# One more pair of heads in cluster order, scatters dealt out by 20 to three steps, and block loads in a fused routing-attention and FFN kernel

## The chip, the cores and the metric

The kernel runs on one NeuronCore of a Trainium2 chip. The metric is device microseconds of one execution, lower is better. Five engines work side by side, each through its own instructions in order: TensorE (PE in the profile; PEld are its weight loads), VectorE (DVE), ScalarE (ACT), GpSimd (POOL) and SyncE (SP), which issues most DMAs.

## The reference

Attention of 4 batches, 8 heads, 768 tokens and head size 64, in which a query sees only keys of its own cluster, followed by a feed-forward network (FFN) with a leaky activation.

```python
q_assign = np.argmax(np.einsum('bhsd,hcd->bhsc', q_n, c_n), axis=-1)   # 16 clusters
k_assign = np.argmax(np.einsum('bhsd,hcd->bhsc', k_n, c_n), axis=-1)
mask = q_assign[:, :, :, None] == k_assign[:, :, None, :]
scores = np.where(mask, scale * np.matmul(q, k.transpose(0, 1, 3, 2)), -1000000000.0)
attn = np.exp(scores - np.max(scores, axis=-1, keepdims=True))
attn = attn / (np.sum(attn, axis=-1, keepdims=True) + 1e-09)
x = np.matmul(attn, v)            # then (B,H,S,D) -> (B*S, H*D) = 3072 x 512
h = x @ w_in                      # 512 x 2048
out = (np.maximum(h, 0.0) + alpha * np.minimum(h, 0.0)) @ w_out   # 2048 x 512
```

## The kernel before, in words

**Pairs and steps.** Two heads fill the 128 partitions; with 4 pairs to a batch there are 16 pairs, numbered 0 to 15. The list `steps` says in which order they are worked on. An ordinary pair is done in two halves of 384 queries (`half` 0 and 1), each in three steps of two key chunks. From step 24 (`TOGETHER`) on, three steps make a group: at its first step (s == 0) TensorE makes the scores of half of the chunks (`score`, L781), sums the denominators of the group before (`total`, L891), weighs the values of the group before (`weigh`, L936, or `weigh_near`, L969), and makes the rest of the scores. ScalarE takes the exponentials (L799, L802), VectorE masks them (`mask`, L822) and adds them up.

**Pairs in cluster order.** From pair `NO` = 10 on, tokens of a pair are sorted by cluster, so that a key chunk meets only a window of the queries: 224, 320 or 384 instead of 768. Such a pair has `half` None and takes one group of three steps in place of two groups. Sorting costs: features turned by VectorE (L565), similarities (`order_sims`, L573), argmax, a scan (L587), two small matmuls (`order_begins`, L599), ranks. Then tokens of q, k and v are loaded into one of two stages (`order_stage`, SP) and 24 indirect DMAs of POOL write them to a scratch in DRAM (`order_scatter`, L673). `order_load` reads them back in order. Afterwards the outcome goes back: transposes (`to_rows`, L999), 12 indirect DMAs (`put_back`, L1008), a load (`fetch_back`, L1020) and `turn_back` (L1027).

**The scatter queue.** The deque `sorting` holds stages and scatters. In every slot (one of 12 places in a group where pieces are put out) up to `room` scatters leave it: one, two in the first step, none where the group before is a pair in cluster order, since its put-backs are then on POOL. With each goes a `pace`: ScalarE copies one element (L649) and POOL copies that (L650), so POOL can't run ahead of ScalarE. The tokens have 8 buffers.

**FFN as filling.** A batch half of the FFN is a list of 28 pieces: 16 of `hidden` (L1063) and 12 of `final` (L1081), each 8 instructions here. They are dealt out evenly over a block of steps between two entries of `begun_at`: batch 1's second half over steps 48 to 59, batch 2's over 60 to 65 and 66 to 77. `kept` holds a few back over the block's end. The last batch's FFN follows after the last step, in a Strassen form (`last_pieces`, products L1241 and L1297, additions L1176, slopes L1181).

**Batch 0.** In the first 24 steps the two weight matrices come as 64-bit words through five raw tiles and are converted by VectorE, ScalarE and POOL (`convert`, L247 to L271). Pairs 0 to 3 are turned into features by TensorE (`prep_features`, L354, copied by ScalarE in L358); later pairs arrive in blocks of 32 features and VectorE turns these (`prep_blocks`, L364). Mask terms of batch 0 ride on the score matmul (L790).

**Order by hand.** `prep_at` and `load_at` say at which step and slot a preparation or load is put out, `ORDERS` at which step each pair's sorting begins, and `later(k, ...)` puts a piece k ticks (slots) on.

```python
    ORDERS = [26, 29, 35, 38, 41, 50]
            room = 0 if steps[u - SB][1] is None else 1 + (s == 0)
        return {NS: 12, begun_at[-2]: 8, begun_at[-3]: 2}.get(block_end(u), 0)
```

Of the kernel before, what the change touches and what calls it, by code (L numbers as in the profile page):

```python
# [19 lines left out]
P = 128  # L20
# [3 lines left out]
def kernel(  # L24
# [77 lines left out]


    pairs = [(b, hp) for b in range(B) for hp in range(NCH)]
    NO = WHOLE * NCH - 2
    NP = len(pairs)
    raw_qk, vts = {}, {}

    Q = 32

    def load(n):

        b, hp = pairs[n]
        for w, src in enumerate((q, k)):
            raw = inp.tile([P, 2, NJ, D], FP32, name="qk")
            if n < NCH:
                nc.sync.dma_start(
                    out=raw.rearrange("p h j d -> p h (j d)"),  # L120
                    in_=src[b, 2 * hp:2 * hp + 2].rearrange("h (p j) d -> p h (j d)",
                                                            j=NJ))
            for h in range(2):
                rows = src[b, 2 * hp + h]
                for x in range(D // Q if n >= NCH else 0):
                    r = h * D + x * Q
                    nc.sync.dma_start(
                        out=raw.rearrange("p h j d -> p (h j d)")[r:r + Q, :].rearrange(
                            "p (t i) -> p t i", i=Q),
                        in_=rows[:, x * Q:(x + 1) * Q].rearrange("(t p) i -> p t i", p=Q))  # L130
            raw_qk[n, w] = raw

    def load_v(n):
        b, hp = pairs[n]
# [189 lines left out]
    lowest = const.tile([P, B], FP32, name="lowest")  # L324
    highest = const.tile([P, B], FP32, name="highest")
    WORDS = [float((127 + e) * 2 ** 23) for e in (-50, 40)]
    kept_of = [0]

    def inverse(n, half):

        if pairs[n][0] > kept_of[0]:
            check_inverses()
        return inverses[:, (2 * n + half) % (2 * NCH), :]

    def check_inverses():
# [343 lines left out]
    def order_load(n):  # L679
        assert len(scattered[n]) == 2 * NX  # L680
        whole = scratch.pop(n)[0]
        found = sorts["order"].tile([P, 2, NJ, 1], I32, name="found")
        for h in range(2):
            r0 = 2 * h * S
            nc.sync.dma_start(out=found[:, h], in_=whole.bitcast(I32)[
# [40 lines left out]
    for b in range(B):  # L726
        whole = [n for n in range(b * NCH, (b + 1) * NCH) if n >= NO]
        rest = [n for n in range(b * NCH, (b + 1) * NCH) if n < NO]
        begun_at.append(len(steps))
        steps += [(n, None, s) for n in whole for s in range(SB)]  # L730
        for half in range(2) if rest else ():
            if half:
                begun_at.append(len(steps))
            steps += [(n, half, s) for n in rest for s in range(SB)]
            feeds[len(steps)] = b, half
    begun_at.append(len(steps))
    assert NJ == 6 and GROUP == 2

# [274 lines left out]
    def fetch_back(n, whole):  # L1013

        b, hp = pairs[n]
        raw = inp.tile([P, 2, NJ, D], FP32, name="qk").rearrange("p h j d -> p (h j d)")
        for h in range(2):
            for x in range(D // Q):
                r = h * D + x * Q
                nc.sync.dma_start(  # L1020
                    out=raw[r:r + Q, :].rearrange("p (t i) -> p t i", i=Q),
                    in_=whole[h * S:(h + 1) * S, x * Q:(x + 1) * Q].rearrange(
                        "(t p) i -> p t i", p=Q))

        def turn_back():
            for half in range(2):
                nc.vector.transpose(out=x_tile(b, half)[:, hp, :],  # L1027
                                    in_=raw[:, half * HS:(half + 1) * HS])
        later(4 if n == NP - 1 else 9, turn_back)

    def x_tile(b, half):
        if (b, half) not in xTs:
# [106 lines left out]
    def last_pieces():  # L1139
# [93 lines left out]
        def hidden(x):  # L1233
# [33 lines left out]

            def p3():
                plus(g_of(f1, 1), product("e", "S4", x_of(1, 1), False))
                slopes(f1)  # L1270

            def p7():
                plus(g_of(f2, 1), product("a", "S3", x_of(1, 0), False))
                late.append(p4)
                if x % 2 == 0 and x:
                    g_sums(x - 2)
# [86 lines left out]
    FREE = SLOTS * SB - 3  # L1363


    ORDERS = [26, 29, 35, 38, 41, 50]
    prep_at, load_at = {}, {}
    for (n, half), u in start_of.items():
        def at(step, slot, piece):
            prep_at.setdefault((step, slot), []).append(piece)  # L1370
        if half is None:
            t = ORDERS[n - NO]
            load_at.setdefault(t, []).append(lambda n=n: load(n))
            for i in range(2):
                at(t + 1, FIRST + i, lambda n=n, i=i: order_features(n, i))
            at(t + 2, 2, lambda n=n: order_sims(n))
            load_at.setdefault(u - (3 if n == NO + 1 else 4), []).append(
                lambda n=n: order_load(n))
            at(u - 4, 0, lambda n=n: prep_clusters(n))
            for i in range(2):  # L1380
# [2 lines left out]
            continue  # L1383
        if half == 0:
            if n < NCH:
                if n > 1:
                    load_at.setdefault(max(u - 7, 0), []).append(lambda n=n: load(n))
                if n > 0:
                    load_at.setdefault(max(u - 6, 0), []).append(lambda n=n: load_v(n))
            else:  # L1390
                load_at.setdefault(u - 9, []).append(lambda n=n: load(n))
                load_at.setdefault(u - 7, []).append(lambda n=n: load_v(n))
            if n < NCH:
                for g in range(len(groups)):
                    at(u - 4, FIRST + g, lambda n=n, g=g: prep_features(n, g))
            else:
                for w in range(2):
                    at(u - 7, FIRST + w, lambda n=n, w=w: prep_blocks(n, w))
            at(u - (3 if n < NCH else 5 if u - 6 < TOGETHER else 6), FIRST,
               lambda n=n: prep_sims(n))  # L1400
            if n >= NCH:
                at(u - 4, FIRST if u - 4 < TOGETHER else 0, lambda n=n: prep_clusters(n))
        if n < NCH:
# [19 lines left out]
    def feed_block(u):  # L1423
        if u == NS:
# [2 lines left out]
                ffn[i] = lambda piece=ffn[i], p=p: (piece(), w_in_sums(p))  # L1427
            ffn.extend(last_pieces())
            return
        ffn.extend(ffn_pieces(*feeds[u]))  # L1430

    def kept(u):


        return {NS: 12, begun_at[-2]: 8, begun_at[-3]: 2}.get(block_end(u), 0)

    def block_end(u):
        return min(x for x in begun_at if x > u)
# [59 lines left out]
    for u in range(TOGETHER, NS + 1):  # L1498
# [54 lines left out]
        for i in slots:  # L1553
# [4 lines left out]
            places = (block_end(u) - block_start(u)) // SB * FREE  # L1558
            pieces = len(ffn) - kept(u) + -whole * (places - 1 - at_slot) // places
            todo.popleft()()  # L1560
            room = 0 if steps[u - SB][1] is None else 1 + (s == 0)
            if room and sorting:
                pace()
            while sorting and room:
# [231 lines left out]
```

## Time and profile before

| What | Value |
|---|---|
| median of 3 runs | 943.94 us (943.76 to 946.52) |
| the profiled execution | 944.23 us, its span 942.5 us |
| PE, DVE, ACT, POOL busy | 924.1, 663.5, 265.9, 351.2 us |
| FFN matmuls L1063, L1081 | 257.7 us (768), 254.4 us (576) |
| score matmuls L781 into sps, values L936 into vps | 88.6 us (480), 87.4 us (480) |
| scatters L673, put-backs L1008 | 155.4 us (144), 74.9 us (72) |
| pace copies L649 on ACT, L650 on POOL | 27.2 us, 55.5 us (196 each) |

Busy time is the union of an engine's instructions; the mean of one can be longer than its share, since instructions overlap in the pipeline. A nc.tensor.matmul in fp32 appears as two instructions. A wait is told as "engine line <- engine line: us, times, longest". The groups of three steps can be found in the timeline by the bursts of L781: from step 24 on they start at 196.6, 223.3, 262.4, 288.1, 323.1, 351.0, 384.4, 412.9, 445.5 (step 48, pair 10), 470.1, 508.2, 531.9, 562.2, 605.6, 643.8 (step 66, pair 12), 671.0, 696.4 and 721.6 us.

### The profile page before, as it was taken

What the parts mean: (1) busy time and instruction counts of PE and PEld (TensorE: products, weight loads), DVE (VectorE), ACT (ScalarE), POOL (GpSimd) and SP (SyncE); (2) the same over time, 40 slices, a digit from 0 to 9 for tenths busy, and PEclk for the clock granted to TensorE, in tenths of its full rate; (3) what the DMA queues carried; (4) which work ended last, traced back from release to release, by engine and by line L of the source; (5) the groups of instructions that cost most, each with busy time, mean ns of one, the idle gap of its engine ahead of it and who ended that gap; (6) DMA issues with size and microseconds to landing.
All of it is one profiled execution on the core that took longest, in us unless ns stands there. A gap on an engine that the chain in (4) does not pass through costs nothing.

```text
span 942.5 us, 11891 instructions
## 1 busy us (share of the span) xinstructions
PE 924.1 (98%) x3995; PEld 496.5 (53%) x3995; DVE 663.5 (70%) x1247; ACT 265.9 (28%) x658; POOL 351.2 (37%) x529
## 2 busy tenths in 40 slices
PE   8999999999999999999999999999999999999997
PEld 5534444445455454454544545545455555556886
DVE  5797788799679589698995955456888535698100
ACT  5764444323123032331322322223133121221000
POOL 2333222200016576467534686364256670000000
PEclk9999999999999999999999999999999999999999
DMA  8333658039001645165920134333441112000000
GB/s 297 125 127 96 146 130 149 18 59 198 1 6 53 159 87 133 47 120 131 155 52 12 43 80 101 63 67 62 93 75 34 32 37 53 1 0 1 23 23 26
DMA packets 209668, 73.38 MB, mean 78 GB/s; under 512 B 194288, under 2 KB 198080, under 8 KB 209600
## 3 DMA queue, kind: packets, MB, share of 16 engines
q1 hardware_dynamic: 201840, 60.35, 29.2%
q0 software_dynamic: 6912, 11.81, 4.1%
q8 instruction: 33, 0.54, 0.2%
q10 hardware_dynamic: 848, 0.39, 0.2%
q14 instruction: 35, 0.29, 0.1%
HBM read 49.89 MB, written 22.28 MB: 77 GB/s over the span
## 4 chain that ended last, share of the span: by engine, by line
PE 87%; DVE 6%; SPq 2%; DMA 2%; issue 1%; POOL 1%; ACT 1%; ACTq 0%; DVEq 0%; POOLq 0%
PE fps L1081 26%; PE fps L1063 25%; PE vps L936 7%; PE sps L781 7%; PE sps L1297 4%; PE sps L1241 4%; PE fps L781 2%; PE vps L1297 2%; PE vps L1241 2%; PE fps L1297 1%; PE fps L1241 1%; PE sps L790 1%; PE vps L969 1%; PE mps L969 1%; PE mps L381 1%
## 5 line engine op out<-in xcount | busy, mean ns | idle before, releaser
L1063 PE MATMUL fps<-xT,w_in_sb 128*128 128x384 f32 x768 | 257.7, 490 | 0.0
L1081 PE MATMUL fps<-w_out_sb,gT 128*128 128x512 f32 x576 | 254.4, 595 | 1.1 <-DVE gT L1055 1.1
L1063 PEld LDWEIGHTS fps<-xT,w_in_sb 128*128 128x128 f32 x768 | 142.8, 190 | 102.6 <-issue 3.8
L1081 PEld LDWEIGHTS fps<-w_out_sb,gT 128*128 128x128 f32 x576 | 107.5, 190 | 133.4 <-issue 123.0
L673 POOL DMA_INDIRECT scratch<-stage,off x144 | 155.4, 1079 | 49.7 <-issue 25.1
L650 POOL COPY paced<-pace 1x1 f32<-1x1 f32 x196 | 55.5, 283 | 202.3 <-ACT pace L649 201.5
L1069 ACT COPY gT<-fps 128x384 f32<-128x384 f32 x96 | 46.0, 479 | 215.6 <-PE fps L1063 215.6
L1055 DVE SCALAR_TENSOR_TENSOR gT<-gT,alpha 128x384 f32<-128x384 f32 x96 | 61.3, 648 | 50.4 <-ACT gT L1069 50.3
L781 PE MATMUL sps<-qkT 64*128 64x384 f32 (+1 forms) x480 | 88.6, 487 | 0.0
L1008 POOL DMA_INDIRECT back<-rows,found x72 | 74.9, 1040 | 18.2 <-issue 16.1
L802 ACT ACTIVATE E<-sps 128x768 f32<-128x768 f32 (+1 forms) x78 | 57.9, 790 | 59.4 <-PE sps L790 38.8
L781 PEld LDWEIGHTS sps<-qkT 64*128 64x128 f32 x480 | 42.7, 186 | 40.5 <-issue 15.0
L822 DVE SCALAR_TENSOR_TENSOR more<-aq,key,more 128x384 f32<-128x384 bf16 (+2 forms) x120 | 63.0, 584 | 1.2 <-ACT more L799 1.1
L936 PE MATMUL vps<-E,vt 128*64 128x384 f32 x316 | 58.6, 495 | 1.4 <-DVE xT L1039 1.4
L904 DVE RECIPROCAL inverses<-mps 64x12 f32<-64x12 f32 (+1 forms) x44 | 10.9, 248 | 58.5 <-PE mps L891 58.1
L822 DVE SCALAR_TENSOR_TENSOR E<-aq,key,E 128x384 f32<-128x384 bf16 (+2 forms) x96 | 50.2, 577 | 1.9 <-ACT E L799 1.8
L271 POOL TENSOR_TENSOR w_in_sb<-w_in_sb,power 128x512 f32<-128x512 f32 x16 | 25.1, 1573 | 67.8 <-DVE w_in_sb L268 67.8
L832 DVE TENSOR_TENSOR acc<-acc,E 128x768 f32<-128x768 f32 x37 | 35.3, 953 | 14.7 <-ACT E L802 13.6
L271 POOL TENSOR_TENSOR w_out_sb<-w_out_sb,power 128x512 f32<-128x512 f32 x16 | 22.9, 1434 | 57.3 <-DVE w_out_sb L268 57.3
L802 ACT ACTIVATE more<-sps 128x768 f32<-128x768 f32 (+1 forms) x42 | 31.1, 775 | 33.1 <-PE sps L781 32.0
L1087 ACT COPY y<-fps 128x512 f32<-128x512 f32 x18 | 10.6, 586 | 99.1 <-PE fps L1081 99.1
L1089 DVE TENSOR_TENSOR y<-y,fps 128x512 f32<-128x512 f32 x24 | 16.4, 683 | 29.1 <-PE fps L1081 29.1
(283 smaller groups left out, 1167.2 us busy)
## 6 DMA issues: line engine op xcount, KB each, us to landing
raw<-in_moe_w_in_dram SPq DMA_DIRECT2D x16, 512.0 KB
raw<-in_moe_w_out_dram SPq DMA_DIRECT2D x16, 512.0 KB
out_dram<-y SPq DMA_DIRECT2D x21, 256.0 KB
qk<-in_q_dram SPq DMA_DIRECT2D x48, 96.0 KB
qk<-in_k_dram SPq DMA_DIRECT2D x48, 96.0 KB
qk<-scratch SPq DMA_DIRECT2D x48, 96.0 KB
w_in_kept<-w_in_sb SPq DMA_DIRECT2D x8, 512.0 KB
vt<-in_v_dram SPq DMA_DIRECT2D x10, 384.0 KB
```

Source lines behind the costliest of these rows:

```text
L650: nc.gpsimd.tensor_copy(out=sorts["paced"], in_=token)
L673: nc.gpsimd.indirect_dma_start(out=scratch[n][1][h * NX + xx], out_offset=bass.IndirectOffsetOnAxis(ap=ranks[n][:, xx, h:h + 1], axis=0), ...
L781: nc.tensor.matmul(out=bank(ps, h, m), lhsT=qkT[r:r + D, S + c * P:S + (c + 1) * P], rhs=qkT[r:r + D, tokens], start=True, stop=not early_ ...
L802: nc.scalar.activation(out=E[:, :, 0:m], in_=ps[:, :, 0:m], func=AF.Exp, scale=SCALE)
L822: nc.vector.scalar_tensor_tensor(out=e, in0=of, scalar=keys[n][:, NJ + c, h:h + 1], in1=e, op0=ALU.is_equal, op1=ALU.mult)
L936: nc.tensor.matmul(out=po[r:r + D, 0:HS], lhsT=vts[n][:, h, c, :], rhs=e[:, h, :], start=(c == 0), stop=(c == NJ - 1))
L1008: nc.gpsimd.indirect_dma_start(out=to[i], out_offset=bass.IndirectOffsetOnAxis(ap=place[:, h, j:j + 1], axis=0), in_=rows[j // HJ][:, j % ...
L1055: nc.vector.scalar_tensor_tensor(out=gs[f], in0=gs[f], scalar=alpha[:, f:f + 1], in1=gs[f], op0=ALU.mult, op1=ALU.max)
L1063: nc.tensor.matmul(out=ps[:, 0:HS], lhsT=w_in_sb[:, c, f * P:(f + 1) * P], rhs=xTs[b, half][:, c, :], start=(c == 0), stop=(c == NCH - 1))
L1081: nc.tensor.matmul(out=ps[:, 0:DM], lhsT=gs[f][:, i * P:(i + 1) * P], rhs=w_out_sb[:, f, :], start=on and f == f0, stop=off and f == f0 + ...
L1241: nc.tensor.matmul(out=bank[to], lhsT=w_in_form(m, x, cc), rhs=rhs[:, cc, :], start=start and cc == 0, stop=cc == KH - 1, skip_group_check ...
L1297: nc.tensor.matmul(out=bank[to], lhsT=g_form(m, x, t), rhs=w_out_form(n, x), start=start and x == 0, stop=x == NQ - 1, skip_group_check=no ...
```

## The change

Pair 9 joins the pairs in cluster order, so batch 2 has three of them and one ordinary pair, 8. There are 75 steps instead of 78. Batch 2's ordinary halves have no block of their own any more: batch 1's second FFN half is dealt over steps 48 to 62, both halves of batch 2's over steps 63 to 74. Scatters leave at up to 2, 1, 2, 1, 2 to the slots of a later step, 20 in a group, and in the last nine steps also beside put-backs. `turn_back` comes 7 ticks after its load instead of 9, some loads a step later, `prep_sims` of pair 8 a slot later. `found` uses the memory of the ranks. `check_inverses` is put out when a batch's inverses are complete, not at the next batch's first. Pair 3 of batch 0 is loaded in feature blocks, by 32 DMAs at steps 2 to 4, and turned by VectorE at step 5. In the last FFN one slope moves from p3 to p7.

```diff
@@ -102,7 +102,7 @@
 
 
     pairs = [(b, hp) for b in range(B) for hp in range(NCH)]
-    NO = WHOLE * NCH - 2
+    NO = WHOLE * NCH - 3
     NP = len(pairs)
     raw_qk, vts = {}, {}
 
@@ -130,6 +130,19 @@
                         in_=rows[:, x * Q:(x + 1) * Q].rearrange("(t p) i -> p t i", p=Q))
             raw_qk[n, w] = raw
 
+    def load_blocks(n, w, h, x):
+
+
+        b, hp = pairs[n]
+        if (h, x) == (0, 0):
+            raw_qk[n, w] = inp.tile([P, 2, NJ, D], FP32, name="qk")
+        rows = (q, k)[w][b, 2 * hp + h].rearrange("(g p j) d -> g p j d", p=Q, j=NJ)
+        r = h * D + x * Q
+        to = raw_qk[n, w].rearrange("p h j d -> p (h j d)")[r:r + Q, :].rearrange(
+            "p (j g i) -> p g j i", g=P // Q, i=Q)
+        for g in range(P // Q):
+            nc.sync.dma_start(out=to[:, g], in_=rows[g][:, :, x * Q:(x + 1) * Q])
+
     def load_v(n):
         b, hp = pairs[n]
         vt = vpool.tile([P, 2, NJ, D], FP32, name="vt")
@@ -324,12 +337,14 @@
     lowest = const.tile([P, B], FP32, name="lowest")
     highest = const.tile([P, B], FP32, name="highest")
     WORDS = [float((127 + e) * 2 ** 23) for e in (-50, 40)]
-    kept_of = [0]
+    kept_of, inverted = [0], [0] * B
 
     def inverse(n, half):
 
-        if pairs[n][0] > kept_of[0]:
-            check_inverses()
+        b = pairs[n][0]
+        inverted[b] += 1
+        if inverted[b] == 2 * NCH and b < B - 1:
+            later(3, check_inverses)
         return inverses[:, (2 * n + half) % (2 * NCH), :]
 
     def check_inverses():
@@ -679,7 +694,8 @@
     def order_load(n):
         assert len(scattered[n]) == 2 * NX
         whole = scratch.pop(n)[0]
-        found = sorts["order"].tile([P, 2, NJ, 1], I32, name="found")
+        found = ranks[n].rearrange("p x h -> p (x h)")[:, 0:2 * NJ].rearrange(
+            "p (h j d) -> p h j d", h=2, d=1)
         for h in range(2):
             r0 = 2 * h * S
             nc.sync.dma_start(out=found[:, h], in_=whole.bitcast(I32)[
@@ -729,10 +745,10 @@
         begun_at.append(len(steps))
         steps += [(n, None, s) for n in whole for s in range(SB)]
         for half in range(2) if rest else ():
-            if half:
+            if half and not whole:
                 begun_at.append(len(steps))
             steps += [(n, half, s) for n in rest for s in range(SB)]
-            feeds[len(steps)] = b, half
+            feeds[len(steps)] = [(b, 0), (b, 1)] if whole else [(b, half)]
     begun_at.append(len(steps))
     assert NJ == 6 and GROUP == 2
 
@@ -1026,7 +1042,7 @@
             for half in range(2):
                 nc.vector.transpose(out=x_tile(b, half)[:, hp, :],
                                     in_=raw[:, half * HS:(half + 1) * HS])
-        later(4 if n == NP - 1 else 9, turn_back)
+        later(4 if n == NP - 1 else 7, turn_back)
 
     def x_tile(b, half):
         if (b, half) not in xTs:
@@ -1267,10 +1283,10 @@
 
             def p3():
                 plus(g_of(f1, 1), product("e", "S4", x_of(1, 1), False))
-                slopes(f1)
 
             def p7():
                 plus(g_of(f2, 1), product("a", "S3", x_of(1, 0), False))
+                slopes(f1)
                 late.append(p4)
                 if x % 2 == 0 and x:
                     g_sums(x - 2)
@@ -1363,7 +1379,7 @@
     FREE = SLOTS * SB - 3
 
 
-    ORDERS = [26, 29, 35, 38, 41, 50]
+    ORDERS = [26, 29, 35, 38, 41, 56, 59]
     prep_at, load_at = {}, {}
     for (n, half), u in start_of.items():
         def at(step, slot, piece):
@@ -1374,7 +1390,7 @@
             for i in range(2):
                 at(t + 1, FIRST + i, lambda n=n, i=i: order_features(n, i))
             at(t + 2, 2, lambda n=n: order_sims(n))
-            load_at.setdefault(u - (3 if n == NO + 1 else 4), []).append(
+            load_at.setdefault(u - (3 if n in (NO + 1, NO + 2, NP - 1) else 4), []).append(
                 lambda n=n: order_load(n))
             at(u - 4, 0, lambda n=n: prep_clusters(n))
             for i in range(2):
@@ -1383,21 +1399,27 @@
             continue
         if half == 0:
             if n < NCH:
-                if n > 1:
+                if n == NCH - 1:
+                    for i in range(4 * D // Q):
+                        at(u - 7 + i // 3, FIRST + i % 3, lambda n=n, i=i: load_blocks(
+                            n, i // (2 * D // Q), i // (D // Q) % 2, i % (D // Q)))
+                elif n > 1:
                     load_at.setdefault(max(u - 7, 0), []).append(lambda n=n: load(n))
                 if n > 0:
                     load_at.setdefault(max(u - 6, 0), []).append(lambda n=n: load_v(n))
             else:
                 load_at.setdefault(u - 9, []).append(lambda n=n: load(n))
                 load_at.setdefault(u - 7, []).append(lambda n=n: load_v(n))
-            if n < NCH:
+            if n < NCH - 1:
                 for g in range(len(groups)):
                     at(u - 4, FIRST + g, lambda n=n, g=g: prep_features(n, g))
             else:
                 for w in range(2):
-                    at(u - 7, FIRST + w, lambda n=n, w=w: prep_blocks(n, w))
+                    at(u - (4 if n < NCH else 7), FIRST + w,
+                       lambda n=n, w=w: prep_blocks(n, w))
             at(u - (3 if n < NCH else 5 if u - 6 < TOGETHER else 6), FIRST,
-               lambda n=n: prep_sims(n))
+               lambda n=n: prep_sims(n)) if u - 6 < 2 * TOGETHER else at(
+                   u - 6, FIRST + 1, lambda n=n: prep_sims(n))
             if n >= NCH:
                 at(u - 4, FIRST if u - 4 < TOGETHER else 0, lambda n=n: prep_clusters(n))
         if n < NCH:
@@ -1427,12 +1449,13 @@
                 ffn[i] = lambda piece=ffn[i], p=p: (piece(), w_in_sums(p))
             ffn.extend(last_pieces())
             return
-        ffn.extend(ffn_pieces(*feeds[u]))
+        for b, half in feeds[u]:
+            ffn.extend(ffn_pieces(b, half))
 
     def kept(u):
 
 
-        return {NS: 12, begun_at[-2]: 8, begun_at[-3]: 2}.get(block_end(u), 0)
+        return {NS: 12, begun_at[-2]: 2, begun_at[-3]: 2}.get(block_end(u), 0)
 
     def block_end(u):
         return min(x for x in begun_at if x > u)
@@ -1558,7 +1581,8 @@
             places = (block_end(u) - block_start(u)) // SB * FREE
             pieces = len(ffn) - kept(u) + -whole * (places - 1 - at_slot) // places
             todo.popleft()()
-            room = 0 if steps[u - SB][1] is None else 1 + (s == 0)
+            room = (0 if steps[u - SB][1] is None and u < NS - 9 else 2 if s == 0 else
+                    1 + (i + 1) % 2)
             if room and sorting:
                 pace()
             while sorting and room:
```

## The prediction

> **What bounds the kernel now.** I read the page first: the engines' busy time, the 40 slices, the chain that ended last.
>
> ```profile
> span 942.5 us, 11891 instructions
> PE 924.1 (98%) x3995; PEld 496.5 (53%) x3995; DVE 663.5 (70%) x1247; ACT 265.9 (28%) x658; POOL 351.2 (37%) x529
> PE   8999999999999999999999999999999999999997
> PE 87%; DVE 6%; SPq 2%; DMA 2%; issue 1%; POOL 1%; ACT 1%; ACTq 0%; DVEq 0%; POOLq 0%
> ```
>
> TensorE is 9 tenths or more in 38 slices and carries 87% of the chain: time follows the TensorE work, plus the few places where TensorE waits. The Trainium skill (Trainium Kernel Development and Optimization, Best Practices) warns that matmul busy time is a poor measure, because matmuls are pipelined; so I also took the distances between the starts of matmuls. They agree here: L1063 comes every 0.32 us and L1081 every 0.43 us in long runs, and all distances above the usual add up to some 14 us in 942.
>
> Next I asked for the stretches that the change touches: 30 to 70 us (batch 0), 445.5 to 562.2 (from the first score of pair 10 to the end of batch 2's first half), 562.2 to 748.7 (to the end of the last score), and the waits of TensorE in the second.
>
> ```profile
> core 0: us, PE busy (x) PEld busy (x) DVE busy (x) ACT busy (x) POOL busy (x), PEclk, DMA share, GB/s
> 30.00:70.00 40.00, 37.04 (x350) 16.40 (x350) 36.96 (x76) 28.16 (x43) 11.44 (x9) 1.00 0.35 111
> 445.50:562.20 116.70, 113.02 (x473) 58.53 (x472) 92.65 (x175) 32.43 (x105) 63.64 (x100) 1.00 0.36 67
> 562.20:748.70 186.50, 186.50 (x731) 97.42 (x732) 124.55 (x231) 48.52 (x151) 97.44 (x145) 1.00 0.34 68
> PE mps L599 <- DVE simT L587: 1.6, 1, 1.6
> PE mps L381 <- DVE qk L975: 1.2, 1, 1.2
> PE mps L969 <- DVE inverses L904: 0.9, 1, 0.9
> ```
>
> Two different regimes: from 30 to 70 us VectorE is as full as TensorE (37.0 of 40); later TensorE is full and VectorE has 20% to 33% spare. The only waits of TensorE near the new pair are these three, all on VectorE; by distances of starts they are 2.1, 1.5 and 1.2 us, 4.7 together.
>
> **What the skill says.** TensorEngine Tiling (Array Packing), Key Properties: tiles of the array work in parallel. The trace agrees: the two heads of a pair, 64 rows each, give 8 score instructions of 384 columns in 1.49 us, 0.19 each, while one alone is modelled at 0.50. So a pair is priced by starts, not by means. DMA: Bandwidth & Descriptors, Specifications, puts full rate at 512 B and more; the new loads of blocks move 128 B pieces. L127's loads have that shape in the trace, and cost SP a median of 0.54 us to issue, 768 pieces each.
>
> **The change, part by part.**
>
> *1. Pair 9 in cluster order (gain).* The chain and TensorE's timeline price a pair:
>
> ```profile
> 534.45 4.02 PE vps L936 x24
> 673.15 1.72 PE vps L969 x16
> 674.87 1.57 PE mps L969 x16
> ...
> 470.06 1.29 PE L781 MATMUL sps<-qkT 64*128 64x224 f32 x8
> 471.19 0.70 PE L781 MATMUL fps<-qkT 64*128 64x320 f32 x4
> 471.83 0.42 PE L891 MATMUL mps<-parts,fold 128*128 128x48 f32 x2
> ...
> 508.18 1.56 PE L781 MATMUL sps<-qkT 64*128 64x384 f32 x8
> 509.57 0.81 PE L781 MATMUL fps<-qkT 64*128 64x384 f32 x4
> 510.31 0.42 PE L891 MATMUL mps<-parts,fold 128*128 128x48 f32 x2
> ```
>
> A half of an ordinary pair: scores 2.13 (508.18 to 510.31) and as much again, weighing 4.02, sum 0.35: 8.65; the pair 17.3. A pair in cluster order: scores 1.77 (470.06 to 471.83) and 1.84, weighing 1.72 + 1.57, sum 0.42: 7.3. It adds six transposes L999 (three in 0.37: 0.75) and four small L599 (0.45); its similarities L573 cost what L381 did. TensorE: 17.3 - 7.3 - 1.2 = **8.8 us less**, on the path because TensorE is full there.
>
> *2. What stands beside it.* The queue of 20 for 14: counting slots by the code, the seven pairs' 168 scatters go 14, 20, 14, 14, 20, 20, 18 to the groups of three steps from step 30 on, then none in 51 to 59, then 14, 20, 14; before 9, 14 x6, 0, 0, 14 x3, 9. So the change does what it says. POOL gains 24 scatters of 1.08 and 12 put-backs of 1.04, 38 us, in an engine that has 63% spare; ScalarE's pace copies fall from 196 to 186. At no cost while a stage is reloaded in time: four scatters 5.2, landing 2.9 (L673's median), three issues of 0.6 (L659), landing some 2.4: 12.3 us for 8 scatters, or 31 for 20, with groups of 26 to 35 us and eight pace tokens, some 10 us, as cover. If the cover goes, ScalarE waits on the token and the exponentials behind it are late: bounds 0 and +11; I take 0. The extra loads on SP (stages, ranks, 10 DMAs of about 0.5) lie in the same spare.
>
> *3. Steps 48 to 62.* FFN of batch 1's second half (28 pieces: 16 of 2.58, 12 of 3.44, 82.6 us) is now spread over 15 steps instead of 12, five groups. TensorE: 82.6 + 3 x 8.05 + 17.3 + similarities, order sums and cluster spreads of 4 = 128 us. VectorE, from its 92.65 of before: less a half of pair 9 (16.2) and its preparation (4.9), plus a pair in order (12 masks 5.7, sums 3.2, turns and row sums 3.9, rest 3.0: 15.8), pair 8's second half 16.2, blocks and queries for two more pairs 8.4, half an ordering 4.7, two turns back 2.2, pair 8's blocks 1.9: 121 us. That is 94% of 128, where before it was 79%. Nothing overflows, but each group start leaves VectorE 1 to 2 us idle, and the last group (order of pairs 14 and 15, blocks of pair 12) asks 30 us of VectorE against 27 of TensorE: behind a late mask stand the row sums, L710's blocks for the next pair, and TensorE's next score. The wait of L381 should go, as `prep_sims` of pair 8 moves a slot later; that of L599 comes twice (pairs 14, 15); that of L969 up to three times; some 2 us at step 63. About 7.7 for 4.7: **+3.0**, bounds -3 and +13 (VectorE at its unpipelined 131 us plus 2 at each of five starts). The turn back after 7 ticks, not 9, has 12 us in a group of 25; fetch to landing took under 7 for pair 12 (712.3 to 719.0), so at most 1 us each, inside that bound.
>
> *4. Steps 63 to 74.* Both halves of batch 2's FFN, 46 pieces in four groups: 43 us of TensorE each against some 27 of VectorE and 35 of POOL. Time is only moved: 0.
>
> *5. Batch 0's last pair.* Removed at step 5: 48 instructions of L354 (42.0 to 46.45, 4.4 us with a wait of 1.5 on ScalarE) and three copies L358 (1.8 us of ScalarE). Added: two VectorE transposes (L364: 0.95 each) and, on SP, 32 loads of 192 pieces for two. VectorE is gapless from 31.7 to 71 us, and TensorE waits for its L1039 at 66.3 (1.7 by starts). So TensorE's 4.4 us become waiting, and VectorE's 1.9 push that point out: **+1.9**. On SP the key blocks stand behind two weight fetches (36.5 and 42.3 us); the last eight are issued by 46.5 and land by 49, when VectorE comes to them. Bounds: -2 (it was TensorE after all), +5 (VectorE waits for the landing).
>
> *6. Slopes in the last FFN.* p3's slopes move behind p7's addition. TensorE waits once there, 1.1 us at 860.3, for L1176, in front of which such slopes stand: **-1.1**, bounds -1.1 and +0.5. `check_inverses`, the shared `found` tile and the loads one step later cost nothing that TensorE sees.
>
> Sum: -8.8 + 3.0 + 0 + 1.9 - 1.1 = **-5.0**. The profiled execution took 944.23 us (span 942.5 and 1.7 around it): 939.2. It lies 0.3 above the median of 943.94, so **939.0**.
>
> **The rivals.** (a) *All of it comes*: batch 0 costs nothing and the waits near pair 9 stay at 4.7: -9.9, 934.0. For it: VectorE never reaches its limit on paper. Against: the gapless VectorE at 30 to 70. (b) *VectorE takes it*: the 13 us of part 3's bound, less the 4.7 that are there already, +8.3, with batch 0 at +1.9: +0.3, 944.2, no change. For it: 94%. Against: from 196.6 to 223.3 VectorE was 25.15 of 26.7 and TensorE lost nothing to it. (c) *Slower, by the stage reload*: 58 scatters fall in the three groups from step 42, which last 86 us (384.4 to 470.1). If the cycle of two stages is 14.7 us instead of 12.3, because SP's loads stand between, they need 107; less 86 and 10 of tokens, ScalarE holds TensorE up for 11: -5 + 11 = +6, **950**. It decides from a cycle of 13.9 us on (no gain left). Against: from 361.3 to 384.0 the trace has 17 scatters in 22.6 us, 8 in 10.7, with one stage wait of 2.5; for: ScalarE already waited for tokens, 7.2 us in five places.
>
> **How the numbers follow.** Forecast 0.50, (a) 0.15, (b) 0.18, (c) 0.17. A measurement of this kernel tells about 0.3%, 2.8 us, from no change: faster means under 941.1, slower over 946.8. The forecast (936 to 942) is nearly all faster, with (a) 0.61; (b) and its edge give 0.21 for the same; (c), with (b)'s tail, 0.18 for slower. The range from 933.5 holds (a); to 947.5 it takes in (b) and the near edge of (c), and leaves out the rest.
>
> **What would show it.** Right: L781 and L936 down by some 10 us over the span, L354 by 48 instructions, TensorE waits between pair 9's first score and pair 12's of about 8 us, a stop before step 10's weighing 2 us later than 68.0. Wrong: pace copies waiting for POOL over 10 us before 470 (c); VectorE over 9 tenths in every slice of steps 48 to 62 with TensorE at 8 (b); or L1039 earlier than 67.4 in batch 0 (part 5).

## The result: slower, by 0.8% at first and 1.9 to 2.0% in two later sets

The kernel after took 952.31 us (median of 4, 952.14 to 953.38) beside 945.23 for the kernel before: ratio 1.0082, 95% interval 1.0068 to 1.0097. In a second set of runs the same program took 964.5 us beside 945.72 (1.0203, 1.0177 to 1.0228) and in a third 962.49 beside 944.9 (1.0186, 1.0168 to 1.0204). The kernel before stayed at 945 in all of them. Of the four executions of e14 below, one, the profiled one, counts as slow (1000.98 us beside 982.81 to 993.79) and is left out of its ratio. The forecast of 939.0 and its range to 947.5 are missed on the slow side.

The page of the first profile after: the engines, and the 40 slices of TensorE and of its clock:

```profile
span 950.6 us, 11882 instructions
...
PE 918.7 (97%) x3915; PEld 493.3 (52%) x3915; DVE 657.8 (69%) x1248; ACT 259.7 (27%) x639; POOL 379.2 (40%) x561
...
PE   8889999999999999999589999999999999999997
...
PEclk9999999999999999999899999999999999999999
```

TensorE's busy time fell by 5.4 us and the span rose by 8.1, so the loss is idle time. One slice shows it: the 20th of 40 (451 to 475 us), 5 tenths. Distances of matmul starts above the usual add up to some 23.7 us, for 9.2 before (both counted in one way): 14.5 more; TensorE's idle time alone grew by 13.5 (31.9 for 18.4). Behind two of the stops TensorE ran at half clock, which costs about 3.6 on top (half of the 3.4 us behind the first; 3.8 busy microseconds behind the second, half of them). 14.5 or 13.5, and 3.6, less 8.1 leave an estimate of 9 to 10 us of work saved: some 3 are the transposes L354 of batch 0 and the rest, some 6, is pair 9.

Busy time by stretch in the kernel after: batch 0, steps 48 to 50 (442.8 to 475.5), steps 48 to 62, steps 63 to 71.

```profile
core 0: us, PE busy (x) PEld busy (x) DVE busy (x) ACT busy (x) POOL busy (x), PEclk, DMA share, GB/s
30.00:70.00 40.00, 34.57 (x290) 13.32 (x288) 35.02 (x72) 25.29 (x38) 11.16 (x8) 0.96 0.46 123
442.80:475.50 32.70, 22.91 (x95) 11.69 (x95) 18.03 (x36) 7.21 (x24) 24.40 (x38) 0.90 0.55 123
442.80:586.80 144.00, 130.72 (x563) 67.76 (x562) 115.05 (x219) 38.59 (x126) 94.07 (x142) 0.96 0.53 96
586.80:713.10 126.30, 125.44 (x465) 66.37 (x464) 77.97 (x151) 27.70 (x90) 75.20 (x115) 1.00 0.41 87
```

In steps 48 to 50 TensorE has 22.9 us of 32.7 and VectorE only 18.0: neither is the bound there, and POOL with 24.4 is the fullest. What TensorE waited for in steps 48 to 62, and the longest of what ScalarE waited for from 430 to 476 us (in the kernel before it waits for no token in that stretch):

```profile
PE sps L797 <- DVE mine L468: 9.8, 1, 9.8
PE mps L985 <- DVE inverses L920: 2.1, 1, 2.1
PE mps L588 <- ACT rows L1018: 0.9, 1, 0.9
PE mps L614 <- DVE simT L602: 0.4, 1, 0.4
```

```profile
ACT pace L664 <- POOL paced L665: 24.7, 12, 3.4
```

The wait of 9.8 us is the stop. VectorE is named, but look at what it waited for itself. The timeline from 462 to 476 us (start, duration, engine; the idle time before it and its releaser in brackets):

```profile
462.49 0.60 SPq L674 DMA_DIRECT2D stage<-in_q_dram  x1
...
464.11 0.19 ACT L664 COPY pace<-ones 1x1 f32<-1x1 f32 x1 [2.50 <-POOL paced L665]
...
465.10 1.11 SPq L701 DMA_DIRECT2D off<-scratch  x2
...
466.32 5.01 SPq L710 DMA_DIRECT2D qk<-scratch  x8
...
469.63 0.19 ACT L664 COPY pace<-ones 1x1 f32<-1x1 f32 x1 [2.76 <-POOL paced L665]
...
471.30 0.98 DVE L726 STREAM_TRANSPOSE qkT<-qk 128x768 f32<-128x768 f32 x1 [9.38 <-DMA qk<-scratch]
...
475.53 1.76 PE L797 MATMUL sps<-qkT 64*128 64x224 f32 x6 [9.82 <-DVE mine L468]
```

Pair 10's `order_load` belongs to step 48, which began at 442.8. SP issues it from 465.1 on, 22 us late, because stage loads (L674) stand ahead of it on the queue and each waits for scatters of POOL. Its data come at 471.3, VectorE turns them, TensorE's first score of step 51 starts at 475.5. Meanwhile ScalarE waits on a token every 2.5 us.

### The profile page after: what moved, and what is told of

The parts are those of the page before. It is cut to its first block, busy times and chain, and to the rows that moved or that the text cites. A ratio compares the mean times of both kernels' runs of the same rounds, so it can differ in the third digit from the quotient of the medians.

```text
span 950.6 us, 11882 instructions
## 1 busy us (share of the span) xinstructions
PE 918.7 (97%) x3915; PEld 493.3 (52%) x3915; DVE 657.8 (69%) x1248; ACT 259.7 (27%) x639; POOL 379.2 (40%) x561
## 4 chain that ended last, share of the span: by engine, by line
PE 87%; DVE 6%; SPq 2%; DMA 2%; issue 1%; POOL 1%; ACT 1%; DVEq 0%; POOLq 0%; ACTq 0%
PE fps L1097 25%; PE fps L1079 24%; PE sps L797 6%; PE vps L952 6%; PE sps L1257 4%; PE sps L1313 4%; PE fps L797 2%; PE vps L1313 2%; PE vps L1257 2%; PE mps L985 1%; PE fps L1257 1%; PE fps L1313 1%; PE vps L985 1%; SPq L710 1%; PE sps L806 1%
## 5 line engine op out<-in xcount | busy, mean ns | idle before, releaser
L688 POOL DMA_INDIRECT scratch<-stage,off x168 | 176.9, 1053 | 85.0 <-issue 37.2
L665 POOL COPY paced<-pace 1x1 f32<-1x1 f32 x186 | 49.7, 267 | 140.7 <-ACT pace L664 140.3
L797 PE MATMUL sps<-qkT 64*128 64x384 f32 (+1 forms) x464 | 86.2, 490 | 10.4 <-DVE mine L468 9.8
L1024 POOL DMA_INDIRECT back<-rows,off x84 | 86.1, 1025 | 21.9 <-issue 16.7
L797 PEld LDWEIGHTS sps<-qkT 64*128 64x128 f32 x464 | 41.8, 188 | 50.0 <-issue 23.7
L838 DVE SCALAR_TENSOR_TENSOR more<-aq,key,more 128x384 f32<-128x384 bf16 (+2 forms) x116 | 60.6, 580 | 0.1
L952 PE MATMUL vps<-E,vt 128*64 128x384 f32 x292 | 55.4, 504 | 1.7 <-DVE xT L1055 1.7
L838 DVE SCALAR_TENSOR_TENSOR E<-aq,key,E 128x384 f32<-128x384 bf16 (+2 forms) x88 | 45.2, 569 | 0.6 <-ACT E L815 0.6
L848 DVE TENSOR_TENSOR acc<-acc,E 128x768 f32<-128x768 f32 x35 | 33.3, 951 | 14.6 <-ACT E L818 13.6
L664 ACT COPY pace<-ones 1x1 f32<-1x1 f32 x186 | 26.6, 185 | 30.1 <-POOL paced L665 30.1
```

Source lines behind the costliest of these rows:

```text
L665: nc.gpsimd.tensor_copy(out=sorts["paced"], in_=token)
L688: nc.gpsimd.indirect_dma_start(out=scratch[n][1][h * NX + xx], out_offset=bass.IndirectOffsetOnAxis(ap=ranks[n][:, xx, h:h + 1], axis=0), ...
L797: nc.tensor.matmul(out=bank(ps, h, m), lhsT=qkT[r:r + D, S + c * P:S + (c + 1) * P], rhs=qkT[r:r + D, tokens], start=True, stop=not early_ ...
L838: nc.vector.scalar_tensor_tensor(out=e, in0=of, scalar=keys[n][:, NJ + c, h:h + 1], in1=e, op0=ALU.is_equal, op1=ALU.mult)
L952: nc.tensor.matmul(out=po[r:r + D, 0:HS], lhsT=vts[n][:, h, c, :], rhs=e[:, h, :], start=(c == 0), stop=(c == NJ - 1))
L1024: nc.gpsimd.indirect_dma_start(out=to[i], out_offset=bass.IndirectOffsetOnAxis(ap=place[:, h, j:j + 1], axis=0), in_=rows[j // HJ][:, j % ...
```

## The experiments

Times are medians. The traces of the runs below, e16 and e17 apart, lack some of the semaphore updates (the signals by which engines and DMAs release each other): the first profile after holds 14174 of them, c2, of the same program, 9590. So starts and durations are read from these traces, and releasers only where they agree.

**Batch 0 alone, and without it.** The kernel before with `load_blocks(3)`, and the kernel after without:

```diff
-                if n == NCH - 1:          # e1_no_blocks; e5 adds these lines to the kernel before
+                if False:
-            if n < NCH - 1:
+            if n < NCH:
```

> The kernel before with the block loads of pair 3 alone. If batch 0 costs what the profile after shows at step 24 (199.6 for 196.6 us), +3.0 us: about 947.8, with the 3.6 us wait for aq at about 43 us and the half clock behind it. If that cost is made up later, since VectorE or the scatters are behind anyway, no change: 944.8.

> The changed kernel with pair 3 of batch 0 loaded and turned as before (TensorE, no block loads). Theory: the block loads cost 3.0 us, all of it before step 12 (batch 0's steps end at 199.6 instead of 196.6 us), so this one takes some 949.3 us and step 24 starts near 196.6; the stop of 10 us before step 51 stays. Rival: the 3 us of batch 0 are given back later because TensorE has other waits there; then it takes 952.3 as the changed kernel does.

e5: 951.43 beside 945.26, ratio 1.0064 (1.0047 to 1.0081), 6.2 us. Step 24 comes 3.4 us later than in a second trace of the kernel before (223.8 to 227.2 at step 27), with a wait of 2.9 us at 49 us for VectorE's blocks and half clock for 6.8; another wait of 2.1 us, for L1102, opens at 796 us, which was not looked for. So by themselves the blocks cost 3 us in batch 0, and more later. e1: 959.79 beside 944.81 (1.0141), not the 949.3 expected: step 24 is back at 196.2, 3.4 us sooner, but the stop at 463 us stays at 10.6 and a new one of 5.6 opens at 596.

**The order of SP's queue.** Pair 10's load two steps earlier, or on ScalarE's queue:

```diff
-            load_at.setdefault(u - (3 if n in (NO + 1, NO + 2, NP - 1) else 4), []).append(
+            load_at.setdefault(u - (5 if n == NO + 1 else 3 if n in (NO + 2, NP - 1) else 4), []).append(
```

```diff
+        queue = nc.scalar if n == NO + 1 else nc.sync      # e6; all of order_load on queue
```

> The changed kernel with pair 10's order_load at step 46 instead of 48. Theory (SP's order): that load stood on SP behind four stage loads which wait for scatters; two steps earlier some three of these are no longer in front of it, it goes out near 447 us instead of 465, and TensorE's stop of 10 us before step 51 and the slow clock after it (some 3 us) go: 939 to 941 us. Rival (VectorE is full, or the scatters of pair 10 are not landed): the load goes out earlier but the stop stays at over 6 us: 948 to 952 us.

> The changed kernel with pair 10's order_load issued by ScalarE's queue instead of SP's, at the same step 48. Theory (SP's order): ScalarE's queue has no stage loads, so the load goes out near 443 us and the stop goes; its 12 issues of about 0.6 us are 7 us of ScalarE in front of step 48's exponentials, so 3 to 6 us of new waits are possible: 940 to 945 us. Rival (data not there, VectorE full): the stop stays: 950 us or more.

e2: 957.97 (1.0131). The load is issued at 443.3 to 447.7 and VectorE no longer waits for it, yet TensorE stops 4.6 us at 470.9 and 2.9 at 625. e6: 964.4 (1.0215); ScalarE's queue needs from 446.3 to 468.4 us to issue the 12 loads, and TensorE stops 18.8 us. The late load was the last wait in the first profile, not the whole cause.

**The rate alone.** The kernel before, its queue at 20 for 14 and nothing else:

```diff
-            room = 0 if steps[u - SB][1] is None else 1 + (s == 0)
+            room = 0 if steps[u - SB][1] is None else 2 if s == 0 else 1 + (i + 1) % 2
```

> The kernel before with nothing but scatters at 2, 1, 2, 1, 2 to the slots of a later step (20 in three steps instead of 14); two pairs of batch 2 in cluster order as before. Theory (SP's order, filled by the rate): up to step 48 there are as many pairs to sort as in the changed kernel, so SP is as late with its stage loads, pair 11's order_load of step 48 stands behind them, and TensorE stops before step 51 (now 470 us) for 6 to 12 us: 951 to 957 us. Rival (the third pair brings the stop, not the rate): no stop, 943.5 to 945 us.

974.64 beside 944.81: 1.0318 (1.03 to 1.0335), **29.8 us**, the largest effect of one line in this study. TensorE's waits between 440 and 640 us:

```profile
PE mps L969 <- DVE highest L340: 5.7, 1, 5.7
PE mps L999 <- DVE simT L402: 5.5, 1, 5.5
PE sps L781 <- issue: 3.5, 4, 1.6
```

Pair 12's `order_load` is issued from 609 us on. TensorE's clock is at half for 19.0 busy us in this stretch, so some 9.5 of the 29.8 (an estimate: half of them) come behind the stops. No pair was added here; so the fast rate has a price by itself in the kernel before. What its price is in the kernel after can't be read from this: e9 and e11 below lower the rate there and gain nothing.

**A rate between, and more tokens.** Rate 17 before step 48; the same with the early load and without the blocks; 16 tokens for 8 with the early load:

```diff
-                    1 + (i + 1) % 2)
+                    1 + (i + 1) % 2 if s == 1 or u >= begun_at[-3] else 1)      # e9, e10
-                           ("xmore", 1), ("byrow", 1), ("pace", 8)):
+                           ("xmore", 1), ("byrow", 1), ("pace", 16)):           # e8
```

> The kernel after with at most 17 scatters for 20 in the groups before step 48 (51 for 58 in the three groups from step 42 come down to 54; the queue is 6 behind at step 45). If the rate is what brings SP and ScalarE late at step 51, SP comes to pair 10's load about 10 us sooner, the 9.9 us stop falls to 2 or less and most of its half clock goes: about 941. If not the rate but the load beside stages and scatters fills the DMA engines, the stop stays near 10 us or moves: 949 to 958.

> Three edits at once on the kernel after: at most 17 scatters before step 48, pair 10's order_load at step 46, pair 3 by feature transposes as before. If rate and SP order are the cause of the stop and batch 0 costs 3: 937 to 939, which is the gain of pair 9 in order. If loads and stages fill the DMA engines wherever they meet: 946 to 958, with a stop of about 5 us at 590 to 600.

> The kernel after with pair 10's order_load at step 46 and 16 pace tokens for 8. If ScalarE, held up by POOL's tokens, is what the early load left behind (30 us of waiting for POOL in the kernel after), the stops at 464 to 475 us and their half clock go: about 941. If tokens only pass on that POOL and its stages are late, or the loads fill the DMA engines, the loss stays or moves: 950 to 958.

967.83 (1.0239), 958.47 (1.0152) and 961.13 (1.0159). None came to 941. In e10 a new thing is seen: from 472.9 to 480.9 us TensorE, VectorE and ScalarE all do nothing, while POOL goes on.

```profile
462.00:471.00 9.00, 8.89 (x62) 5.13 (x61) 8.61 (x18) 2.64 (x7) 7.48 (x12) 1.00 0.28 77
472.90:480.90 8.00, 0.00 (x0) 0.00 (x0) 0.00 (x0) 0.00 (x0) 6.45 (x11) 0.61 0.47 124
```

**Both kernels once more.** All variants were slower than expected, so the two kernels were run again, unchanged.

> The kernel after, unchanged, as a yardstick beside the next two on one chip. If the variants so far were slower than it by their edits: 952. If the place of the long stop is a matter of chance, because three queues (SP, POOL, ScalarE's tokens) run near their limit there: 953 to 962, with stops at other places than 465 us.

> The kernel before, unchanged, built once more as the variants were, to see what a second build of one program is worth. If the place of the long stops in the kernel after is chance in itself (its second build took 964.5, its first 952.3), this one stays at 945. If every second build is slower, whatever the program (semaphore updates are missing from those traces, and not from the first two), this one is at 950 to 958, and variants are to be compared with second builds alone.

The kernel after took 964.5, 12 us more than at first; the kernel before 945.71 beside 945.3 (0.9999, 0.9989 to 1.0009). The spread belongs to the kernel after: in c1 its stops are 3.4 us at 451, 4.4 at 471, 2.8 at 481 and three of 0.7 to 1.2 around 600 with half clock, so step 63's group lasts 52.5 us, for 44.8 in the first profile. One more thing sets the first profile apart: it holds all the updates, and c1 and c2 don't. For the kernel before that makes no difference (its first profile, 944.23 us, holds all, c0's, 945.5 us, does not); whether it does for this kernel was not tested. Variants are compared with 962 to 964 from here on. Against that e1, e2 and e10 gain some 3 to 6 us, e8 little, and e9 loses 3 to 5.

**The rate of before, with what is left over beside the put-backs.**

```diff
-            room = (0 if steps[u - SB][1] is None and u < NS - 9 else 2 if s == 0 else
-                    1 + (i + 1) % 2)
+            room = (int(s > 0) if steps[u - SB][1] is None and u < NS - 15 else 2 if s == 0 else
+                    1 if u < NS - 15 else 1 + (i + 1) % 2)
```

> The kernel after with the rate of before, 14 scatters in a group, up to step 59; the ones that this leaves over go out one to a slot in the second and third steps of the groups at 51, 54 and 57 (10, 10 and 7), beside the put-backs. 9 and 14 for the 14 and 20 in the groups at 30 and 33, 42 for 58 in the three from step 42. Theory: a backlog in the scatter queue (POOL behind its tokens, stages and SP behind POOL) brings the stops and the halts of all three engines at 450 to 490; then they go, and 939 to 943 is left (batch 0's 3 us included). Rival: it is the cluster-ordered pairs side by side and their loads, whatever the rate; then a stop of 5 to 11 us stays between 450 and 490: 950 to 960.

> The same, with pair 10's order_load two steps earlier and pair 3 by feature transposes as before: the pair in cluster order with neither of the two costs found so far. If the queue's backlog is the cause: 936 to 940. If not: 946 to 956.

979.86 (1.0361) and 976.11 (1.0309): worse than either theory said. The stop near 475 us falls to 2.2, as the first theory has it, but stops open where the scatters went: 7.0 us at 505, 1.6 at 536, 4.8 at 549. In these runs the scatters that were left over brought stops in their new place too.

**Reloads, tokens, small pieces.** Four kernels on one chip; e13 leaves out the stage loads after the first two (it scatters old data), e15 puts tokens in the wrong places:

```diff
+        if i >= STAGES or n > NO:                  # e13, in order_stage
+            return
-            if room and sorting:                   # e14
-                pace()
-                        in_=whole[r0:r0 + S, x * Q:(x + 1) * Q].rearrange("(t p) i -> p t i", p=Q))
+                        in_=whole[r0 + x * (S // 4):r0 + (x + 1) * (S // 4)].rearrange("(p a) d -> p (a d)", p=Q))
```

> The kernel after, unchanged, a third time, as the yardstick of this call. 952 or 964, as one of the two sets before, if its stops lie where they lay there; a value between or beyond if their place is chance.

> The kernel after with the reload of the stages left out: only the first two parts of pair 9 are loaded, all 168 scatters go out, of old data. SP issues 162 loads less and no scatter waits for a stage. If the cycle of the two stages (scatters, landing, reload) is the bound near step 51, as rival (c) had it, POOL keeps up, the stops at 450 to 490 us and around 595 go and what is left is batch 0: 941 to 944. If POOL's scatters or the loads in order cost by themselves, stops of 5 us or more stay: 950 or above.

> The kernel after without the pace copies that go with the scatters (102 on ScalarE, 102 on POOL), those of the put-backs stay. ScalarE is never held up by POOL for a scatter. If the tokens hand POOL's delay to TensorE, as rival (c) had it: 942 to 946. If the delay comes through SP (loads behind the stages) anyway: as the yardstick, within 3 us, with the stop at 465 to 475.

> The kernel after with the eight loads of q and k in order_load in 32 pieces each for 768, of the same bytes (so the tokens stand in the wrong places). If a flood of small pieces fills the DMA engines and halts everything: 940 to 946, and no stops near 470 and 595. If the stages and POOL are the cause: as the yardstick, within 3 us.

c2, the yardstick: 962.49. e13: 955.19, 7.3 us less, not 20 (6 stage loads are left of 126, so 120 fewer, not the 162 of the expectation). e15: 960.1, no difference that the spread of 957 to 965 lets tell. e14: 1.0443, by the two ratios 24 us more than c2. In c2, e13 and e15 all three engines stand still from some 455 us on, for 11.3, 9.9 and 11.2 us. So neither the reload nor the small pieces make that halt. The stretch before it, the halt and the stretch behind it in c2:

```profile
438.50:451.00 12.50, 12.50 (x54) 5.69 (x52) 8.36 (x15) 2.58 (x7) 10.21 (x19) 1.00 0.29 84
455.50:466.00 10.50, 0.00 (x0) 0.00 (x0) 0.00 (x0) 0.00 (x0) 7.44 (x13) 0.61 0.35 105
466.00:478.00 12.00, 11.11 (x22) 5.12 (x23) 8.68 (x19) 2.50 (x11) 8.07 (x12) 0.77 0.96 176
```

POOL issues 19 scatters in one chain from 438.5 to 463.5, 1.39 us apart, and the halt ends 1.9 us after the last. ScalarE's next instruction in it is no pace copy but an exponential, L815, of scores that TensorE had begun at 451.15 and left; it came 18.6 us after ScalarE's last work:

```profile
466.40 0.77 ACT L815 ACTIVATE E<-fps 128x320 f32<-128x320 f32 x2 [18.56 <-remote]
```

VectorE's next, L1055 at 466.4, also waits for TensorE alone. The matmuls that both wait for ended by 452.0. Those that ended from 451.2 to 455.1 carry five updates of TensorE's semaphore; in the trace five updates of it stand together at 466.3 to 466.5, and none between. The same clump of five ends the halts of e13, e14 and e15. In the traces that hold all updates (before, the first after, e16) none of TensorE's comes over 0.05 us behind its matmul. So in these halts TensorE's signals are late, and that was seen only in traces that lack updates. Full DMA engines aren't needed for it, 0.35 of them were busy in c2's halt, but they were full in e13's:

```profile
454.50:464.30 9.80, 0.00 (x1) 0.00 (x0) 0.00 (x0) 0.00 (x0) 6.90 (x13) 0.68 1.06 196
```

Without the paces (e14, the profile is of its longest execution) the same appears at another place, where no variant had it: a chain of 20 from 289.2 to 314.8, and

```profile
289.00:301.50 12.50, 12.50 (x63) 6.23 (x61) 11.85 (x23) 3.24 (x6) 9.67 (x11) 1.00 0.38 120
302.00:318.00 16.00, 0.00 (x0) 0.00 (x0) 0.00 (x0) 0.00 (x0) 10.77 (x14) 0.65 0.33 103
318.50:330.00 11.50, 11.09 (x27) 6.13 (x28) 8.41 (x18) 3.10 (x6) 0.00 (x0) 0.77 0.00 0
```

The kernel before has no chain of nine scatters or put-backs under 1.7 us apart, and no halt before its end.

**Fewer tokens.** If chains make the halts, three tokens, which keep POOL at most six scatters behind, should shorten both:

```diff
-                           ("xmore", 1), ("byrow", 1), ("pace", 8)):
+                           ("xmore", 1), ("byrow", 1), ("pace", 3)):
```

> The kernel after with 3 pace tokens for 8. New theory: POOL issuing scatters back to back (10 to 20 of them, 1.35 us apart) halts TensorE, VectorE and ScalarE, whose semaphore updates arrive only when POOL pauses; the backlog that makes such a chain is what 8 tokens allow (up to 16 scatters). With 3 tokens POOL can be 6 scatters behind at most, so chains stay short and the halts go: 944 to 952, against 952 to 964 of the kernel after, with ScalarE's waits for POOL longer (over 30 us). If the tokens only hold ScalarE and the halts have another cause, fewer tokens make it worse: 965 or above.

> The same with pair 10's order_load two steps earlier and pair 3 by feature transposes, the best version in sight. By the new theory: 937 to 946. If the halts stay, 955 or above.

973.65 (1.0307) and 962.55 (1.0187): by its own yardstick the theory failed. All three engines stand still for 6.9 us at most (2.6 in e17). But these two traces hold all updates, so their like is the first profile after, where that is 2.8 us with eight tokens: that fewer tokens shorten the halts is not shown. What is shown is that ScalarE is now held at POOL's pace. ScalarE's waits for tokens from 400 to 500 us, then TensorE's from 400 to 610, both in e16:

```profile
ACT pace L664 <- POOL paced L665: 59.3, 22, 12.0
```

```profile
PE fps L797 <- ACT gT L1085: 19.1, 3, 10.1
PE fps L797 <- DVE y L1105: 2.1, 1, 2.1
```

Over the whole span ScalarE waits 121 us for POOL, for 30 in the first profile after and 7 before. Fewer tokens lengthen ScalarE's waits. Early load and no blocks together give 11.1 us here (e16 to e17) and 9.4 in e9 to e10. No version came under the kernel before.

## Why the prediction was wrong, by its own steps

**Part 2 is the step that failed.** It reads "At no cost while a stage is reloaded in time" and takes 0 of 0 to +11. The cycle itself was sized well: stage loads follow each other from 438.6 to 462.5 us in four intervals of 6.0, so 12.0 for 8 scatters, where 12.3 was worked out. What was wrong is the comparison. Part 2 made it for one group ("31 for 20, with groups of 26 to 35 us") with the tokens as cover each time. Over the three groups from step 42 on it is 58 scatters x 12.0 / 8 = 87 us. Rival (c) did set the 58 against these three groups, but against their 86 us in the kernel before, with the tokens' 10 us on top. The change itself made them shorter, by putting FFN pieces later: from 387.4 to 475.5 they last 88.1 us in the first profile after, and 78 without the stop of 9.8. So 87 us stand against 78, and the cover of one delay is not there for the next: when step 51 began, POOL had issued 108 of the 120 scatters due. And "63% spare" was POOL's share of the whole span; in chains a scatter takes 1.35 us from start to start, not 1.08, so 58 take 78 us, all of that time, before any wait. The rate alone, on the kernel before, costs 29.8 us (e7), nearly three times the upper bound. How much of the loss in the kernel after is the rate's can't be separated.

**SP and ScalarE** were both given spare as well. Pair 10's load came 22 us late behind stage loads, and ScalarE's token waits, 24.7 us from 430 to 470, pass rival (c)'s mark of 10. Rival (c), at 950, named the place and the sign and was near the first measurement, which is in part luck: the mechanism it gave, a cycle of 14.7 us with a turning point at 13.9, was not what happened, since the loss came at 12.0. Leaving the reload out altogether gives back 7.3 of the 17.6 us that c2 loses. It had 0.17.

**Part 1** had its mechanism right. (Its 8.65 for a half of a pair adds up to 8.63, which changes nothing.) L781 and L936 go from 197.8 to 188.0 us, 9.8 down, as "some 10" said; in-order weighing adds 3.3, transposes 0.7, by distances of starts. By the balance above some 6 of the 8.8 us are there; the exact rest can't be separated from the half clock.

**Part 3** was mis-sized with it: 128 us of work and 7.7 of waits became 144.0. Of these 130.7 are busy, some 1.9 of it by half clock, so the work was sized well; 13.3 are waits, 9.8 of them the stop. VectorE was not what filled it, 115 of 144 against 121 of 128; rival (b) falls with that.

**Part 4** held in the first profile (125.4 of 126.3 us busy) and not in c1, where the halt near 600 us falls into it. **Part 5** took +1.9 and measured +3.0 at step 24 (199.6 for 196.6), within its bounds: the last key blocks land at 50.8, not by 49, and TensorE waits 3.5 us for `aq`, a small load issued by ScalarE at 42.8 that lands at 47.5, among the blocks; without them (e1) that wait is gone. The step-10 weighing came at 71.06, three later than 68.02 where two were foretold. **Part 6** took 1.1 and gave 0.3: the stop at 860 fell from 0.9 to 0.6.

**What stays open** is why TensorE's signals are late in a chain of scatters, so that three engines stand still. Every time on record comes with a clock and a span of the profiler. The kernel after took 952 where the trace holds all updates and 962 to 964 where it lacks some, and no run tells whether what loses the records also holds the signals back, or the chains do both. The Trainium skill (SBUF — State Buffer, SBUF: two separate sides) says that VectorE and GpSimd share a pair of ports which one of them holds for a whole instruction, and that TensorE and ScalarE never wait on it; by itself that would not hold ScalarE for 18.6 us, and no run here tests it. A chain doesn't always halt them: e12 has two of 17 with no standstill of all three over 2 us, and the first profile after has one of 20 from 602.9 to 629.0 us with none, while c1 stops near 600 behind one of 12, in a group that is 7.7 us longer, most of what separates 964 from 952. Which chains do was not found.

## What to carry to other kernels

Compare a producer's demand with its capacity over the busiest stretch of consecutive groups, as long as these are after the change, at the spacing it has when it runs without pause, and not over the span or for one group. Once there is no slack, every queue behind it (loads issued in order, tokens, engines) gets its delay in turn, so mending the wait that ended last (e2) moved it. Before weighing variants of a kernel at such a limit, run it twice: its medians here lay 12 us apart, those of the kernel before 1.2.

## What the runs showed of the hardware that was not expected

The three halts shown at length (e10, c2, e14) lie in unbroken chains of 16 to 20 indirect DMAs, or end just behind them, and lasted 8 to 17 us, with the DMA engines at a share of 0.33 to 0.47, so not full. In c2, e13, e14 and e15, whose traces lack some updates, TensorE's signals of finished work come together at the end of the halt, in c2 over 11 us after the work.

TensorE's clock falls to 0.50 some 2 to 6 us after a stop begins and stays there for 3.413, 6.827, 10.24, 13.653, 17.067 (e14, e16) or 20.48 us (e6), past the restart; the 12 scores behind the stop of 9.8 us took 3.4 us (475.53 to 478.92) for 1.77. The Trainium skill (TensorE: Matmul & The Clock Gate, Part 1: The HAM clock gate) describes a half clock after an idle window of about 3.4 us; these durations, one to six times 3.413, agree. A stop is thus dearer than its length, by some 2 us behind the longest ones (half of the 3.8 to 5.0 us that TensorE still ran at 0.50 behind those of the first profile, c2, e6 and e14).
